# Two weight transfers issued earlier, a low-rank product in another PSUM bank, and one cast split over two engines

## The chip, the cores and the metric

The kernel runs on one core of one Trainium2 chip. The metric is the device time of one execution in microseconds (us), smaller is better. TensorE is called PE here (its weight loads PEld), VectorE DVE, ScalarE ACT, GpSimd POOL and SyncE SP. Each engine works through its own list of instructions in order; DMA transfers are issued from the lists of SP and POOL and run beside the engines.

## The reference

Two operators follow one another: a retention recurrence over 4 batches and 8 heads, and a mixer with a low-rank product over time and an MLP over channels.

```python
# q, k, v: (4, 8, 768, 64); gamma has one value for each head
for t in range(S):
    state = gamma[None, :, None, None] * state + einsum('bhd,bhe->bhde', k[:, :, t], v[:, :, t])
    y[:, :, t] = scale * einsum('bhd,bhde->bhe', q[:, :, t], state)
x = y.transpose(0, 2, 1, 3).reshape(B, S, H * D)          # (4, 768, 512)

xt = x.transpose(0, 2, 1)
h = xt @ U @ V                                            # U (768, 32), V (32, 768)
u = x + h.transpose(0, 2, 1)
out = u + relu(u @ w_ch1) @ w_ch2                         # w_ch1 (512, 2048), w_ch2 (2048, 512)
```

## The kernel before

The 768 steps of a batch are cut into six chunks of 128 (NCK is 6). Inside a chunk the recurrence is done as masked scores (k times q) multiplied with v, and across chunks as a running state multiplied with q. The powers of gamma are put on q and v when these are cast to bf16. Batch 0 has code of its own (the functions whose names end in `_early`) and works in three blocks of 256 steps, with q and k turned by PE. Batches 1 to 3 go by chunks, with q and k turned by DVE (`turn_chunk`, line 302). While PE does the MLP of batch b-1, the recurrence of batch b is put between the pieces of that MLP: `weave` takes a list of MLP pieces (`up`, line 452, and `down`, line 482) and a list of marks, each a share of the MLP at which a piece of other work is emitted.

The order on every engine is written out by hand: an engine executes its instructions in the order in which the Python code emits them. What the change and the steps of the prediction touch is this.

**Batch 0.** `cast_early` casts one block of q, k or v. Its last arguments say which engine takes which heads: ("P", 4, 4) gives heads 4 to 7 to POOL, ("D", 4, 4) gives them to DVE. `turn_early` then turns the block on PE (line 555) and copies it out of PSUM (`kt`, `qt`), `score_early` makes the scores (line 577) and masks them on DVE (`a`, line 582).

**The loads of batch 1.** All of them are issued by SP in this order: the first half of k (`kin`, eight transfers of 96 KB, line 107), the first half of q (`qin`), v of chunks 0 to 2 (256 KB each, line 116), the second half of k, and v of chunks 3 to 5. The second half of q has its eight transfers issued by POOL instead (line 107 too), in groups of 3, 3 and 2 between its casts. A half holds three chunks.

**The weights.** w_ch1 goes into the tile `w1b` in four transfers (`load_w1(0)` to `load_w1(3)`, line 280, 512 KB each as bf16), w_ch2 into `w2b` in four more (line 285). All eight are issued by POOL. `load_w1(0)` and `load_w1(1)` are issued during batch 0. The other two stand between the casts of batch 1's first chunk.

**The casts of batch 1.** POOL casts k (`ki`, line 83), q (`qi`, line 85) and v (`vd`, line 85) of each chunk, and each cast waits for the load of its data. In the order of before, POOL's list runs: the constants (lines 217 to 222), `ki` of chunk 0, `load_w1(2)`, `qi` of chunk 0, `load_w1(3)`, `vd` of chunk 0, `ki` and `qi` of chunk 1, three transfers of `qin`, `vd` of chunk 1, three more of `qin`, `ki`, `qi` and `vd` of chunk 2, two more of `qin`, two of `w2b`, `ki` of chunk 3, `qi` of chunk 3, and so on. `qi` of chunk 3 is the first that needs the second half of q.

**PSUM.** There are eight banks: `R[0]` and `R[1]` hold two each and carry scores, mixing and the low-rank product; three banks of the tag `mlp` are handed out in turn by `bank("mlp")`; one holds the state. `lr_proj(b)` multiplies x with U (24 matmuls, line 400) and copies the product `pc` out with DVE. Before the change it writes into the second bank of `R[1]`. In the first MLP, `lr_proj(1)` is emitted close behind `lr_expand(0, 0, 4)` (line 409), whose result in `R[0]` and `R[1]` is read by two additions on DVE (`u`, line 416).

Of the kernel before, what the change touches and what calls it, by code (L numbers as in the profile page):

```python
# [16 lines left out]
def kernel(  # L17
# [12 lines left out]
    P = 128  # L30
    B, H, S, D = q.shape
# [28 lines left out]
    R = [psum.tile([P, 2, 512], fp32, tag=f"r{g}", name=f"r{g}") for g in range(2)]  # L60

    def bank(tag, dtype=fp32):
        n_bank[0] += 1
        return psum.tile([P, 2048 // (4 if dtype == fp32 else 2)], dtype,
                         tag=tag, name=f"{tag}_{n_bank[0]}", bufs=BANKS[tag])
# [4 lines left out]
    def evac(eng, dst, src):  # L70
        if eng == "A":
            nc.scalar.activation(dst, src, AF.Copy)  # L72
        else:
            nc.vector.tensor_copy(out=dst, in_=src)

    def cast(eng, dst, src, scale=None):
        if eng == "A":
            assert scale is None
            nc.scalar.activation(dst, src, AF.Copy)
            return  # L80
        e = nc.vector if eng == "D" else nc.gpsimd
        if scale is None:
            e.tensor_copy(out=dst, in_=src)  # L83
        else:
            e.tensor_tensor(dst, src, scale, op=ALU.mult)  # L85
# [33 lines left out]
    def feed_more(n=0):  # L119
        allowed[0] += n  # L120
        while n_fed[0] < len(feed) and n_held[0] < RING and allowed[0] > 0:
            nm, b, i = feed[n_fed[0]]
            if nm == "T" and n_cast[b - 1] < NCK * (i + 1):
                return
            n_fed[0] += 1
            allowed[0] -= 1
            if nm == "T":
                load_turned("k", b, i)
                load_turned("q", b, i)
            else:  # L130
                load_natural(nm, b, i)
# [95 lines left out]
    def late_exps():  # L227
        nc.scalar.activation(gk, pos, AF.Exp, scale=-1.0)
        nc.scalar.activation(gqT, posT, AF.Exp)
# [3 lines left out]
    def prep_turned(nm, b, ci, eng="P"):  # L233
        src = turned_in[nm, b, ci // HC][:, :, ci % HC].rearrange("p h (a j d) -> p h a j d", a=2,
                                                   j=2)
        t = rpre.tile([P, 2, 2, D, 2], bf16, tag=nm + "i", name=f"{nm}i_{b}_{ci}")
        scale = None
        if nm == "q":
            scale = gqT[:, ci].rearrange("p h (a j) -> p h a j", a=2)
            scale = scale[:, :, :, :, None].to_broadcast([P, 2, 2, 2, D])  # L240
        cast(eng, t.rearrange("p h a d j -> p h a j d"), src, scale)
        pre[nm + "T", b, ci] = t
        n_cast[b] += 1
        feed_more()

    def prep_natural(nm, b, ci, eng="P"):
        t = rpre.tile([P, H, D], bf16, tag=nm + "d", name=f"{nm}d_{b}_{ci}")
        scale = None
        if nm == "v":
            scale = gk[:, ci, :, None].to_broadcast([P, H, D])  # L250
        cast(eng, t, take(nm, b, ci).rearrange("p (h d) -> p h d", h=H), scale)
        pre[nm, b, ci] = t
        feed_more()
# [25 lines left out]
    def load_w1(mb):  # L279
        nc.gpsimd.dma_start(  # L280
            out=w1b[:, :, ts(mb, 512)],
            in_=moe_w_ch1[:, ts(mb, 512)].rearrange("(c p) n -> p c n", p=P))
# [111 lines left out]
            pre.pop(("v", b, n))  # L394

    def lr_proj(b):
        p_p = R[1][:, 1]
        for j in range(NCK):
            for c in range(NCB):
                nc.tensor.matmul(p_p[ds(RK * c, RK), :P], Ub[:, j],  # L400
                                 xs[b][:, j, ts(c, P)], start=(j == 0),
                                 stop=(j == NCK - 1))
        pcs[b] = rmid.tile([P, P], bf16, tag="pc", name=f"pc_{b}")
        evac("D", pcs[b], p_p[:, :P])
# [128 lines left out]
    def home(shape, name):  # L533
        return rin.tile(shape, bf16, tag="in", name=name)
# [3 lines left out]
    def cast_early(nm, B0, *pieces):  # L538
        t = eb[nm, B0] = home([P, 2, H, D], f"{nm}b_{B0}")
        g = {"q": gq2, "k": None, "v": gk2}[nm]  # L540
        for eng, h0, nh in pieces:
            hs = ds(h0, nh)
            scale = None
            if g is not None:
                scale = g[:, B0, hs].rearrange("p h j -> p j h")
                scale = scale[:, :, :, None].to_broadcast([P, 2, nh, D])
            src = early[nm, B0][h0 // 4][:, ds(h0 % 4, nh)]
            cast(eng, t[:, :, hs], src.rearrange("p h (j d) -> p j h d", j=2), scale)

    def turn_early(nm, B0, engines="A"):  # L550
        src = eb[nm, B0]
        tp = bank("mlp", bf16)
        for hp in range(4):
            for j in range(2):
                nc.tensor.transpose(tp[:, ts(2 * hp + j, P)],  # L555
                                    src[:, j, ds(2 * hp, 2)], ident)
        t = eb[nm + "T", B0] = home([P, 4, 2 * P], f"{nm}t_{B0}")
        if nm == "k":
            evac(engines, t.rearrange("p n m -> p (n m)"), tp)
            return  # L560
        dst = t.rearrange("p n (t j) -> p n j t", j=2)
        src = tp.rearrange("p (n j t) -> p n j t", n=4, j=2)
        if len(engines) == 1:
            evac(engines, dst, src)
        else:
            for f in range(2):
                evac(engines[f], dst[:, ds(2 * f, 2)], src[:, ds(2 * f, 2)])
# [112 lines left out]
    state_early(3)  # L680
    load_w1(0)
    turn_early("q", 2)
    cast_early("k", 2, ("P", 0, 4), ("P", 4, 4))
    turn_early("k", 2, "D")
    cast_early("v", 2, ("P", 0, 4), ("D", 4, 4))
    load_uv()
# [14 lines left out]
    p_p = bank("mlp")  # L701
# [38 lines left out]
    for lo in range(2):  # L740
        for g in range(2):
            evac("AD"[g], uTs[0][:, ds(2 * g, 2), ts(lo, 256)], R[g][:, :, ts(lo, 256)])
    late_exps()
    prep_turned("k", 1, 0)
    load_w1(2)
    prep_turned("q", 1, 0)
    load_w1(3)
    prep_natural("v", 1, 0)
    prep_turned("k", 1, 1)
    prep_turned("q", 1, 1)  # L750
# [19 lines left out]
    for b in range(1, B):  # L770
# [22 lines left out]
        def mixed():  # L793
            if b > 1:
                lr_open(b)
            lr_proj(b)
# [41 lines left out]
```

## Time and profile before

| | us |
|---|---|
| median of 6 executions | 234.57 |
| lowest and highest of the 6 | 233.42 and 235.48 |
| the profiled execution, its own time | 234.04 |
| its span in the profile, first to last instruction | 232.3 |
| PE busy | 211.5 |
| DVE busy | 107.7 |
| POOL busy | 96.7 |
| ACT busy | 76.9 |
| mean granted TensorE clock | 0.993 of full |

The span is 1.7 us shorter than the time of the same execution; the rest lies outside the first and last instruction. All places in time below are counted from the start of the span. A line number such as L85 is a line of the kernel printed above, and `out<-in` after it names the tiles that an instruction writes and reads. A wait is written as "who waited <- who ended the wait". In a table of stretches (windows), the columns are the stretch, its length, the busy time of PE, PEld, DVE, ACT and POOL with the number of instructions in brackets, the granted TensorE clock as a share of full, the mean busy share of the 16 DMA engines (over 1 where packets overlap), and GB/s moved. A DMA's time "to landing" runs from its issue to the signal that its data is there.

### The profile page before, as it was taken

To read this page: it belongs to the slowest core of one execution; us is meant where nothing else is said; L and a number is where in the kernel's file an instruction comes from. 1 tells how busy PE (TensorE), PEld (TensorE's weight loads), DVE (VectorE), ACT (ScalarE), POOL (GpSimd) and SP (SyncE) were. 2 spreads that over 40 slices of the span, in tenths; PEclk is the share of its full clock that TensorE was granted. 3 is DMA by queue.
4 is the path that set the end of the run, shared out by engine and by line. 5 is a ranking of instruction groups with operands and counts; after the bars stand their busy time and mean duration, and the time that the engine had idled before them with its cause. 6 is when DMAs were issued, how large, how long until landed. Compare 5 with 4: busy or idle time off the path is not lost.

```text
span 232.3 us, 5794 instructions
## 1 busy us (share of the span) xinstructions
PE 211.5 (91%) x2411; PEld 123.0 (53%) x2437; DVE 107.7 (46%) x194; ACT 76.9 (33%) x174; POOL 96.7 (42%) x141
## 2 busy tenths in 40 slices
PE   0799799977979999999999999999999999999991
PEld 0577467635734444568644444577544444774451
DVE  5667546625566226765345255566416152222121
ACT  2355456653410005556320025566110044540000
POOL 4687559939502249199057401991011100001110
PEclk9999999997999999999999999999999999999999
DMA  6999979999942599997771768930023530001212
GB/s 175 290 291 235 262 178 223 273 207 233 228 133 93 130 222 254 217 250 193 180 148 45 181 180 211 259 86 0 3 93 81 144 90 0 3 0 45 93 61 74
DMA packets 65738, 35.21 MB, mean 152 GB/s; under 512 B 41920, under 2 KB 63808, under 8 KB 65712
## 3 DMA queue, kind: packets, MB, share of 16 engines
q1 hardware_dynamic: 59200, 23.64, 44.4%
q0 software_dynamic: 6512, 11.21, 19.4%
q8 instruction: 19, 0.31, 0.6%
q14 instruction: 7, 0.06, 0.1%
HBM read 30.90 MB, written 6.29 MB: 160 GB/s over the span
## 4 chain that ended last, share of the span: by engine, by line
PE 31%; issue 31%; DMA 13%; POOL 13%; SPq 9%; DVE 1%; POOLq 0%; DVEq 0%
PE mlp L482 15%; PE mlp L452 11%; DMA v<-in_v_dram 6%; DMA qin<-in_q_dram 4%; SPq L107 4%; POOL out_dram L441 3%; POOL qi L85 3%; SPq L163 3%; SPq L165 3%; DMA kin<-in_k_dram 3%; POOL vd L85 2%; POOL ki L83 2%; POOL qin L107 2%; PE r L369 1%; PE r L350 1%
## 5 line engine op out<-in xcount | busy, mean ns | idle before, releaser
L452 PE MATMUL mlp<-uT,w1b 128*128 128x256 bf16 (+1 forms) x517 | 89.0, 323 | 1.0 <-ACT uT L72 0.4
L482 PE MATMUL mlp<-w2b,gT 128*128 128x512 bf16 (+2 forms) x385 | 84.0, 370 | 1.5 <-issue 0.8
L459 ACT ACTIVATE gT<-mlp 128x256 bf16<-128x256 f32 (+1 forms) x90 | 42.8, 479 | 87.3 <-PE mlp L452 85.9
L452 PEld LDWEIGHTS <-w1b 128*128 128x128 bf16 x528 | 50.5, 99 | 31.7 <-issue 1.1
L482 PEld LDWEIGHTS <-gT 128*128 128x128 bf16 x400 | 37.4, 98 | 42.3 <-issue 0.4
L441 POOL DMA_DIRECT2D out_dram<-o x24 | 13.3, 556 | 93.1 <-DVE o L489 93.1
L489 DVE TENSOR_TENSOR o<-mlp,u 128x512 f32<-128x512 f32 (+2 forms) x25 | 16.7, 669 | 47.1 <-PE mlp L482 47.1
L384 DVE TENSOR_TENSOR a<-r,mask 128x512 bf16<-128x512 f32 x36 | 23.2, 686 | 25.3 <-ACT x L72 21.0
L457 DVE TENSOR_SCALAR gT<-mlp 128x256 bf16<-128x256 f32 (+1 forms) x42 | 22.8, 545 | 21.4 <-PE mlp L452 21.3
L85 POOL TENSOR_TENSOR qi<-qin,gqT 128x512 bf16<-128x512 f32 x18 | 18.9, 1048 | 3.6 <-DMA qin<-in_q_dram 3.6
L85 POOL TENSOR_TENSOR vd<-v,gk 128x512 bf16<-128x512 f32 x18 | 18.8, 1042 | 2.0 <-DMA v<-in_v_dram 0.7
L72 ACT ACTIVATE x<-r 128x256 bf16<-128x256 f32 x36 | 11.9, 381 | 23.3 <-PE r L369 14.8
L416 DVE TENSOR_TENSOR u<-r,x 128x512 bf16<-128x512 f32 (+1 forms) x16 | 14.6, 952 | 7.7 <-PE r L409 7.7
L83 POOL CAST kd<-k 128x512 bf16<-128x512 f32 x12 | 7.3, 609 | 19.6 <-DMA k<-in_k_dram 19.6
L83 POOL CAST ki<-kin 128x512 bf16<-128x512 f32 x18 | 13.8, 765 | 3.4 <-DMA qin<-in_q_dram 2.1
L369 PE MATMUL r<-qT,kT 32*128 32x128 bf16 x288 | 7.1, 215 | 2.9 <-DVE qT L302 2.9
L302 DVE STREAM_TRANSPOSE qT<-qi 128x256 f32<-128x256 f32 x18 | 7.3, 408 | 3.9 <-POOL qi L85 3.9
L302 DVE STREAM_TRANSPOSE kT<-ki 128x256 f32<-128x256 f32 x18 | 7.9, 437 | 2.3 <-POOL ki L83 2.3
L555 PE MATMUL mlp<-ident,qb 128*128 128x128 bf16 x24 | 3.5, 310 | 5.9 <-DVE qb L85 5.7
L350 PEld LDWEIGHTS <-a 128*128 128x128 bf16 x144 | 6.7, 100 | 2.4
L582 DVE TENSOR_TENSOR a<-r,mask 128x1024 bf16<-128x1024 f32 x6 | 7.1, 1219 | 1.2 <-PE r L577 1.2
L350 PE MATMUL r<-vd,a 128*128 128x64 bf16 x144 | 7.3, 196 | 0.0
(82 smaller groups left out, 131.3 us busy)
## 6 DMA issues: line engine op xcount, KB each, us to landing
v<-in_v_dram SPq DMA_DIRECT2D x24, 256.0 KB, 5.5
out_dram<-o POOLq DMA_DIRECT2D x23, 256.0 KB, 2.4
kin<-in_k_dram SPq DMA_DIRECT2D x48, 96.0 KB, 5.0
qin<-in_q_dram SPq DMA_DIRECT2D x40, 96.0 KB, 3.0
k<-in_k_dram SPq DMA_DIRECT2D x12, 256.0 KB, 4.8
w1b<-in_moe_w_ch_dram POOLq DMA_DIRECT2D x4, 512.0 KB, 8.7
w2b<-in_moe_w_ch_dram POOLq DMA_DIRECT2D x4, 512.0 KB, 10.4
qin<-in_q_dram SPq DMA_DIRECT2D x2, 512.0 KB, 5.8
```

What stands on the lines that cost most here:

```text
L83: e.tensor_copy(out=dst, in_=src)
L85: e.tensor_tensor(dst, src, scale, op=ALU.mult)
L302: nc.vector.transpose(out=dst, in_=src)
L350: nc.tensor.matmul(R[g][:, hp % 2, ds(256 + D * i, D)], a[:, 2 * hp + i], vb[:, 2 * hp + i], start=(i == 0), stop=True, skip_group_check=True)
L384: nc.vector.tensor_tensor(a[:, ds(4 * g, 4)].rearrange("p (n i) m -> p n i m", n=2), R[g][:, :, :256].rearrange("p n (i m) -> p n i m", i= ...
L416: nc.vector.tensor_tensor(v4(us[b][:, ds(j0, nj), e]), R[g][:, :, :nj * P].rearrange("p c (j e) -> p c j e", j=nj), v4(xs[b][:, ds(j0, nj) ...
L441: nc.gpsimd.dma_start(out=dst, in_=src)
L452: nc.tensor.matmul(g_p[:, :sz], w1b[:, c, ts(m, P)], uTs[b][:, c, ds(lo, sz)], start=(c == 0), stop=(c == NCB - 1))
L457: nc.vector.tensor_relu(gT[:, m, ds(lo, sz)], g_p[:, :sz])
L459: nc.scalar.activation(gT[:, m, ds(lo, sz)], g_p[:, :sz], AF.Relu)
L482: nc.tensor.matmul(ch[:, :nn], gT[:, m, ts(j, P)], w2b[:, m, ds(n0, nn)], start=(m == 0), stop=(m == NM - 1))
L489: nc.vector.tensor_tensor(o_sb, ch[:, :nn], us[b][:, j, n], op=ALU.add)
```

## The change

It has three parts, and none changes what is computed.

1. `load_w1(2)` is emitted ahead of `ki` of batch 1's chunk 0, and `load_w1(3)` ahead of `qi` of that chunk. Each moves forward past one cast on POOL's list.
2. `lr_proj` writes its product into a bank handed out by `bank("mlp")` in place of the second bank of `R[1]`. This holds for batches 1, 2 and 3.
3. The cast of k of batch 0's last block is split: heads 0 to 3 stay on POOL, heads 4 to 7 go to DVE.

```diff
     def lr_proj(b):
-        p_p = R[1][:, 1]
+        p_p = bank("mlp")
         for j in range(NCK):
             for c in range(NCB):
                 nc.tensor.matmul(p_p[ds(RK * c, RK), :P], Ub[:, j],
...
     turn_early("q", 2)
-    cast_early("k", 2, ("P", 0, 4), ("P", 4, 4))
+    cast_early("k", 2, ("P", 0, 4), ("D", 4, 4))
     turn_early("k", 2, "D")
...
     late_exps()
+    load_w1(2)
     prep_turned("k", 1, 0)
-    load_w1(2)
+    load_w1(3)
     prep_turned("q", 1, 0)
-    load_w1(3)
     prep_natural("v", 1, 0)
```

## The prediction

> **What bounds the kernel now.** I read the page first, then PE's waits, then the chain of waits from 24 to 60 us, then POOL in order of time, then the DMA load by stretches.
>
> ```profile
> span 232.3 us, 5794 instructions
> PE 211.5 (91%) x2411; PEld 123.0 (53%) x2437; DVE 107.7 (46%) x194; ACT 76.9 (33%) x174; POOL 96.7 (42%) x141
> ```
>
> PE is busy 91% of the span, so time is gained only where PE waits. Its waits between 20 and 75 us:
>
> ```profile
> PE r L369 <- DVE qT L302: 2.9, 1, 2.9
> PE r L400 <- DVE u L416: 1.5, 1, 1.5
> ```
>
> These are the two largest once the start is over, and after 75 us the waits of PE itself come to 0.6 us. So parts 1 and 3 matter only through what comes before the first MLP and through the 2.9, part 2 through the 1.5. Where the 2.9 comes from is told by the chain:
>
> ```profile
> 31.20 3.66 DMA v<-in_v_dram
> 34.86 0.08 issue
> 34.95 1.03 POOL vd L85
> ...
> 44.76 0.52 POOL qin L107
> 45.29 6.57 DMA qin<-in_q_dram
> ...
> 52.16 1.05 POOL qi L85
> 53.22 0.02 issue
> 53.24 0.46 DVE qT L302
> 53.70 0.04 issue
> 53.74 0.40 PE r L369 x16
> ```
>
> The load of v for chunk 0 lands, POOL then works without a hole from 34.95 until it has issued the last `qin` transfer at 45.29, that transfer takes 6.57, and `qi`, `qT` and PE follow. The lead of the chain is v of chunk 0. POOL around the moved transfers:
>
> ```profile
> 30.56 0.76 POOL L83 CAST ki<-kin 128x512 bf16<-128x512 f32 x1 [2.15 <-DMA qin<-in_q_dram]
> 31.24 0.82 POOL L280 DMA_DIRECT2D w1b<-in_moe_w_ch_dram  x1
> 32.90 1.04 POOL L85 TENSOR_TENSOR qi<-qin,gqT 128x512 bf16<-128x512 f32 x1 [0.85 <-DMA qin<-in_q_dram]
> 33.89 0.80 POOL L280 DMA_DIRECT2D w1b<-in_moe_w_ch_dram  x1
> 34.95 1.03 POOL L85 TENSOR_TENSOR vd<-v,gk 128x512 bf16<-128x512 f32 x1 [0.26 <-DMA v<-in_v_dram]
> ```
>
> It idles for 2.15, 0.85 and 0.26 us, each time for a load. The last columns of these stretches are DMA share and GB/s:
>
> ```profile
> 28.00:30.00 2.00, 1.63 (x16) 1.45 (x15) 1.17 (x3) 1.78 (x6) 0.35 (x2) 1.00 1.07 280
> 30.00:32.00 2.00, 2.00 (x23) 1.61 (x25) 0.74 (x2) 1.13 (x3) 1.44 (x2) 1.00 0.54 152
> 32.00:34.00 2.00, 1.95 (x18) 0.94 (x19) 1.65 (x3) 0.40 (x2) 1.15 (x3) 1.00 0.86 176
> 36.00:40.00 4.00, 4.00 (x52) 3.28 (x49) 3.05 (x7) 2.15 (x6) 3.98 (x6) 1.00 1.24 230
> ```
>
> The engines of the DMA have a lull at 30 to 34 us, and are full from 34 to 64 (1.1 to 1.3 in every stretch).
>
> **Part 2, the bank.** PE comes to L400 at 68.08 and starts it at 69.62, since the second addition `u`, which reads the bank, ends at 69.56. In an `mlp` bank the product need not wait: two of the three are held by the two open `down` products, the third was last read by a relu before 62 us, and x was copied out at 66.5. Gain 1.54. What is queued behind: the copy of `pc` (0.29) still stands behind `u` on DVE and ends near 69.9; `lr_expand`, the first to need it, would come at 70.4. The next `down` takes a free bank at 70.8; should it be given the first one, its sum `o` (0.69, after `pc`) is out at about 70.6. Next late is the last `w2b` transfer, landed at 66.63 and needed at 68.6, so 1.9 us of cover. Bounds: 0 if one of these takes over, -1.54 if none. I take -1.5, as each has a margin. For batches 2 and 3 nothing: PE has no wait at L400 there, and a free bank is used again no sooner than one whole `down` later (16 matmuls, over 3 us).
>
> **Part 3, the cast.** A half of k takes POOL about 0.59 (1.18 for two) and DVE 0.38 (0.76 for two in block 0). The second half ends at 19.48 on POOL now. On DVE it starts when the mask products end, 19.28, and is done at 19.66. PE's last four transposes come 0.2 later, as does `kt`: it would end at 21.05 and not 20.87. Behind it on DVE stands `vb`, which waits for its load until 21.18 (0.31 of idle), so the delay is covered. Without that cover it costs 0.2. POOL's 0.6 buys nothing, as its next cast, `vb` at 20.02, already waits 0.54 for a load. Bounds -0.1 to +0.2; I take 0.
>
> **Part 1, the transfers.** POOL is free at 28.41. `load_w1(2)` (0.82) moves from 31.24 to 28.41, into the hole of 2.15 ahead of `ki`; `load_w1(3)` (0.80) moves from 33.89 to 31.24, into the hole that is there ahead of `qi`. Neither delays a cast by its issue. `vd` is freed of 0.80 of issue ahead of it, but waits for v anyway, so POOL gains nothing. Nor does PE wait for `w1b` in the trace. What changes is the order of the data on the DMA engines:
>
> (a) A gain. The lull is filled: (1.2 - 0.54) x 2 + (1.2 - 0.86) x 2 = 2.0 us of share, over 1.2, or 1.7 us. All that is queued behind can land up to 1.7 earlier, the last `qin` included.
>
> (b) A loss. w1 would now move beside the end of q's first half and v of chunk 0, the head of the chain. The nearest rows are the v loads themselves, asked for one by one: v of chunk 0, issued at 31.20, lands in 3.7 us, before w1 gets going; v of chunk 1, issued at 31.70 and overlapped by `load_w1(2)`, takes 7.4; v of chunk 2, overlapped by both, 10.5. A v load is 262 KB, 1.0 us at the 250 GB/s of full stretches. So one w1 transfer delays a v load behind it by 7.4 - 3.7 - 1.0 = 2.7 us, two by about 10.5 - 3.7 - 2.0 = 4.8. In the new order v of chunk 0 would meet `load_w1(2)` after about a third of it has moved (issued 2.8 ahead of v), two thirds of 2.7 or about 2.0 us.
>
> Here a rule speaks against the change. The Trainium skill, "DMA: Bandwidth & Descriptors", Queues, rings and completion order, says that each DMA engine takes turns between the queues that have work, a packet at a time. Taking turns by descriptor, a v load has 1024 pieces of 256 B, w1 pieces of 1 KB; each piece of v would then wait for one of w1, all of both transfers, 1.05 MB or 4.2 us at 250 GB/s (an estimate from that page and the stretch rows), and the sum would be 2.2 higher than by the row. Taking turns by equal bytes, v waits for 262 KB, 1.0 us, and the sum is 1.0 lower. The row of v of chunk 1 lies between; I use it, and keep 0 and 4.8 as the ends.
>
> From v of chunk 0 on POOL has no hole, so 2.0 us late there is 2.0 late at the last `qin` issue. That transfer took 6.57 among full DMA engines (6.5 to 7.1 for all eight); with 1.7 us less queued it should take about 4.9. PE restarts 2.0 - 1.7 = 0.3 later. Bounds for the restart: -1.7 (no loss) to +4.8 (no gain); taken +0.3.
>
> **A second price on the same wait.** The stretch table by single microseconds gives a granted clock of 0.59, 0.50, 0.50 and 0.70 from 55 to 59 us, after the wait of 2.92: 1.7 us of full clock lost. The Trainium skill, "TensorE: Matmul & The Clock Gate", Part 1, lets the clock fall after an idle window of about 3.4 us; by that alone a wait of 2.9 costs no clock. The trace decides: it did, and the wait of 1.54 at 68 us did not. So with +0.3 the loss stays as it is and adds 0; were the wait cut to about 1.6, another 1.7 would come back (by the rule, nothing).
>
> **The sum.** -1.5 + 0 + 0.3 = -1.2. Against the profiled execution's 234.04 that is 232.8; it ran 0.5 under the median of 234.57, so on the median 233.4.
>
> **The rivals.** Half a percent, 1.17 us, is about what a measurement of this kernel can tell from no change: faster means under 233.4, slower over 235.7.
>
> A, likeliest, 0.45: as summed, 233.4, its own range 232.3 to 234.6; 0.20 faster, 0.23 same, 0.02 slower.
>
> B, 0.22, faster: v of chunk 0 is hardly touched, because its transfers are on their way before w1's are prepared. PE restarts 1.3 earlier: 231.8, and 230.1 if the clock no longer falls. For: `load_w1(2)` took 7.1 us to land, so it starts slowly. Against: it will be issued 2.8 us ahead of v.
>
> C, 0.25, slower: `load_w1(3)` follows `load_w1(2)` without a break, and v of chunk 0 gets through only behind both. It lands 4.8 late, near 39.7; POOL, and the `qin` issues on it, are late by that; less the 1.7, PE restarts 3.1 later: 234.57 - 1.5 + 3.1 = 236.2, and 237.9 with a second fall of the clock. It turns slower than the bound once the restart is over 2.7 late, that is, when v of chunk 0 lands after 39.3. For: the 10.5 of v of chunk 2. Against: the DMA can turn to v between the two. Chances 0.04 same, 0.21 slower.
>
> D, 0.08: part 2 gives nothing because the last `w2b` or a bank is late: 234.9; 0.06 same, 0.02 slower.
>
> Together 0.42 faster, 0.33 same, 0.25 slower. The range of 230.5 to 236.8 leaves out the best end of B and the worst of C.
>
> **What would show it.** Right: no wait at L400 near 68; `w1b` issues at 28.4 and 31.2; v of chunk 0 landing at 36 to 38 and `vd` following it; the last `qin` in about 5 us; PE's wait for `qT` near 3 us and the fall of the clock after it; `kt` 0.2 later with no trace on PE. Wrong: `vd` still at 35 (B), or after 39 (C), or a wait for a bank or `w2b` at 68 to 71 (D), or a PE wait after 75 us that is not there now.

## The result and the profile after

By its ratio to the kernel before, 1.0002 with a 95% interval of 0.998 to 1.0024, the change makes no difference that the measurement can tell. The median of all 35 executions is 236.17 us, against 234.45 of 72 of the kernel before. The ratio is formed from the executions within 1.5% of the fastest of their own kernel (14 of the 35, 63 of the 72), so it leaves out most of the long ones, of which the changed kernel has more: 21 of its 35 took over 236 us, against 4 of the 72.

The profiled execution took 232.52 us, the shortest of the 35. It shows what the change can do at its best. The page and PE's waits between 20 and 75 us:

```profile
span 230.7 us, 5794 instructions
PE 213.0 (92%) x2411; PEld 123.7 (54%) x2437; DVE 108.0 (47%) x195; ACT 77.1 (33%) x174; POOL 96.1 (42%) x140
```

```profile
PE r L369 <- DVE qT L302: 2.3, 1, 2.3
PE mlp L452 <- ACT uT L72: 0.4, 1, 0.4
PE mlp L314 <- DVE kT L302: 0.2, 1, 0.2
...
```

The wait of 1.5 us at L400 is gone, the wait for `qT` is still there. POOL in order of time, around the moved transfers:

```profile
28.50 0.81 POOL L280 DMA_DIRECT2D w1b<-in_moe_w_ch_dram  x1
30.94 0.76 POOL L83 CAST ki<-kin 128x512 bf16<-128x512 f32 x1 [1.62 <-DMA kin<-in_k_dram]
31.62 0.77 POOL L280 DMA_DIRECT2D w1b<-in_moe_w_ch_dram  x1
35.89 1.05 POOL L85 TENSOR_TENSOR qi<-qin,gqT 128x512 bf16<-128x512 f32 x1 [3.50 <-ACT uT L72]
36.90 1.04 POOL L85 TENSOR_TENSOR vd<-v,gk 128x512 bf16<-128x512 f32 x1
```

Both issues sit in holes, as intended. But `qi` of chunk 0 starts at 35.89 and not at 32.90, and `vd` at 36.90 and not at 34.95. The name behind the 3.50 (ACT `uT`, done long before) is not what ended that wait: the last transfers of q's first half landed only at 35.8, by their issue and landing times in the trace, where they had landed at 32.8. The load of v of chunk 0 took 5.4 us (3.7 before) and was in at 36.7, while POOL was still at `qi`: here it is q, not v, that holds `vd` back.

The load of the DMA engines, with share and GB/s in the last two columns, shows the lull filled:

```profile
30.00:32.00 2.00, 2.00 (x20) 1.67 (x18) 0.85 (x2) 1.02 (x3) 1.06 (x2) 1.00 1.04 189
32.00:34.00 2.00, 1.95 (x17) 0.92 (x17) 1.54 (x3) 0.52 (x2) 0.39 (x1) 1.00 1.17 219
```

The end of the chain to PE's restart, and then the place of the product, from the chain of waits:

```profile
47.22 4.72 DMA qin<-in_q_dram
...
52.25 1.05 POOL qi L85
53.30 0.02 issue
53.32 0.46 DVE qT L302
53.78 0.04 issue
53.82 0.40 PE r L369 x16
```

```profile
67.36 0.81 PE mlp L482 x3
68.17 0.45 PE mlp L400 x24
68.62 1.83 PE mlp L482 x8
```

The last `qin` transfer is issued 1.9 us later than before and takes 4.72 in place of 6.57, so PE restarts at 53.82 against 53.74: 0.1 later. The product follows the matmuls before it without a hole. In this execution 0.1 is lost and 1.5 gained, and the span is 1.6 shorter. The question is why most executions do not keep that.

### The profile page after: what moved, and what is told of

Same layout as the page of the kernel before. It is cut to its first block, busy times and chain, and to the rows that moved or that the text cites. A ratio compares the mean times of both kernels' runs of the same rounds, so it can differ in the third digit from the quotient of the medians.

```text
span 230.7 us, 5794 instructions
## 1 busy us (share of the span) xinstructions
PE 213.0 (92%) x2411; PEld 123.7 (54%) x2437; DVE 108.0 (47%) x195; ACT 77.1 (33%) x174; POOL 96.1 (42%) x140
## 4 chain that ended last, share of the span: by engine, by line
PE 35%; issue 30%; SPq 15%; DMA 9%; POOL 7%; DVE 2%; POOLq 0%; ACT 0%; DVEq 0%
PE mlp L452 13%; PE mlp L482 13%; SPq L107 7%; DMA u<-in_k_dram 3%; POOL out_dram L441 3%; SPq L116 2%; DMA qin<-in_q_dram 2%; SPq L163 2%; SPq L424 2%; DMA kin<-in_k_dram 2%; SPq L165 2%; POOL qi L85 2%; DMA v<-in_v_dram 2%; POOL vd L85 1%; PE r L369 1%
## 5 line engine op out<-in xcount | busy, mean ns | idle before, releaser
L459 ACT ACTIVATE gT<-mlp 128x256 bf16<-128x256 f32 (+1 forms) x90 | 42.8, 479 | 86.0 <-PE mlp L452 84.7
```

The source lines that it names most:

```text
L459: nc.scalar.activation(gT[:, m, ds(lo, sz)], g_p[:, :sz], AF.Relu)
```

## The experiments

### Each part alone

Part 2 alone (`e1_bank`), part 1 alone (`e2_w1`), parts 2 and 3 (`e3_bank_cast`), and part 3 alone (`e9_cast`), each against the kernel before. The diffs are the pieces of the change shown above.

Part 2 alone:

> Part 2 alone (the product in a bank of its own). Theory G (given back: the bank saves its 1.5 us, and the earlier weight transfers cost about as much in the timed executions, though they cost 0.1 in the profiled one): ratio 0.992 to 0.996, and no wait at L400. Rival N (the bank saves nothing at the end, because a later wait takes its place, and the transfers are neutral): 0.998 to 1.002, with a new PE wait after 70 us. Rival K (bank and transfers as predicted, but the split cast costs over 1 us): 0.992 to 0.996 here too.

Measured: ratio 0.9952 (0.9924 to 0.9979), median 233.19 of 22 executions against 234.16. There is no wait at L400 in its list of PE's waits, and none takes its place after 70 us. The first line of that list from 20 to 75 us:

```profile
PE r L369 <- DVE qT L302: 1.8, 1, 1.8
```

So the bank is worth about 1.1 us (0.48% of 234.16), inside what theory G gave and somewhat under the 1.5 that one trace shows; that 1.5 is inside the interval. Rival N is out.

Part 1 alone:

> Part 1 alone (load_w1(2) ahead of the k cast, load_w1(3) ahead of the q cast). Theory G: slower, ratio 1.004 to 1.012, the wait of 1.5 us at L400 back, and in the profile v of chunk 0 landing at 36 us or later. Rival N: 0.998 to 1.002. Rival K: 0.999 to 1.003.

Measured: ratio 1.0072 (1.0037 to 1.0107), median 237.14. POOL in order of time:

```profile
28.85 0.81 POOL L280 DMA_DIRECT2D w1b<-in_moe_w_ch_dram  x1
31.04 0.76 POOL L83 CAST ki<-kin 128x512 bf16<-128x512 f32 x1 [1.38 <-DMA kin<-in_k_dram]
31.72 0.77 POOL L280 DMA_DIRECT2D w1b<-in_moe_w_ch_dram  x1
35.93 1.04 POOL L85 TENSOR_TENSOR qi<-qin,gqT 128x512 bf16<-128x512 f32 x1 [3.44 <-DMA qin<-in_q_dram]
37.33 1.04 POOL L85 TENSOR_TENSOR vd<-v,gk 128x512 bf16<-128x512 f32 x1 [0.35 <-DMA v<-in_v_dram]
```

Here the profile names the loads: `qi` waits 3.44 us for q, then `vd` 0.35 more for v, which lands at 37.2. The wait at L400 is back at 1.5 us. Part 1 costs 1.7 us by the ratio (0.72% of 234.16; 0.9 to 2.5 by the interval) and 3.0 by the medians of all executions (237.14 against 234.16). By the ratios the two parts nearly cancel. By the medians they do not: -1.0 and +3.0 us, and the whole change +1.7. Either way part 1 gives back at least about what part 2 gains, and theory G stands.

Parts 2 and 3:

> Parts 2 and 3 without part 1. Theory G: as part 2 alone within 0.2%, ratio 0.992 to 0.996. Rival N: 0.998 to 1.002. Rival K: about 1.000, that is 0.4% or more over part 2 alone, with the masks of the last block later on DVE by over 1 us.

Measured: 0.9972 (0.9947 to 0.9998), median 232.89. The ratio is 0.2% over that of part 2 alone, the median 0.3 us under it, and the intervals overlap over more than half of their width. No difference from part 2 alone is shown.

Part 3 alone:

> Part 3 alone. Theory: nothing, ratio 0.998 to 1.002, since DVE's cast ends 0.2 us later than POOL's did and vb on DVE waits for its load anyway. Rival K (the split cast costs): 1.002 to 1.005, the masks of the last block on DVE starting over 0.3 us later than the load of v explains.

Measured: 0.9999 (0.9972 to 1.0026). No effect of the cast shows, and of rival K's range (1.002 to 1.005) all but the lowest end lies outside the interval.

### Which of the two transfers

`e4_one_w1` puts `load_w1(3)` back behind the q cast, `e10_w1_3_early` puts `load_w1(2)` back behind the k cast. Both keep parts 2 and 3.

```diff
     load_w1(2)
     prep_turned("k", 1, 0)
-    load_w1(3)
     prep_turned("q", 1, 0)
+    load_w1(3)
```

> The changed kernel with load_w1(3) put back behind the q cast: only load_w1(2) is early. Theory G with its cause in the second transfer (v of chunk 0 gets through only behind both): faster, ratio 0.992 to 0.996, v of chunk 0 landing at 35 to 37 us. Theory G with its cause in load_w1(2) alone: 0.998 to 1.003, as the whole change. Rival N: 0.998 to 1.002.

Measured: 1.0116 (1.0072 to 1.016), median 236.58 of 6. None of the expectations held: with one early transfer fewer, it is no faster than the whole change. By the ratio it is slower; the medians of all executions (236.58 of these 6, 236.17 of the 35) are too near to show that. Its POOL and PE:

```profile
36.16 1.04 POOL L85 TENSOR_TENSOR qi<-qin,gqT 128x512 bf16<-128x512 f32 x1 [4.22 <-ACT uT L72]
37.15 0.81 POOL L280 DMA_DIRECT2D w1b<-in_moe_w_ch_dram  x1
37.98 1.05 POOL L85 TENSOR_TENSOR vd<-v,gk 128x512 bf16<-128x512 f32 x1
```

```profile
PE r L369 <- DVE qT L302: 4.8, 1, 4.8
```

`load_w1(2)` alone makes q's first half late (`qi` at 36.16). `load_w1(3)` now stands behind that late `qi` and is issued at 37.15, where it was at 33.89. It is under way until about 45, beside the first six transfers of q's second half, which take 7.0 to 8.5 us (5.3 to 6.0 in the profile of the whole change). The last `qin`, issued at 48.29 when `load_w1(3)` had landed, still took 7.5 us; what slowed that one is not shown. Nothing of the lateness is won back.

```diff
-    load_w1(2)
     prep_turned("k", 1, 0)
+    load_w1(2)
     load_w1(3)
     prep_turned("q", 1, 0)
```

> The changed kernel with load_w1(2) put back behind the k cast, so that only load_w1(3) is early (directly behind load_w1(2), ahead of the q cast). Theory V2 (load_w1(2), which starts before v of chunk 0 is on its way, does the harm): v of chunk 0 lands at about 35 us as before, ratio 0.992 to 0.998. Rival V3 (the two in one row do it, wherever the first stands): v of chunk 0 lands after 37, ratio 0.999 to 1.008.

Measured: 1.0012 (0.9979 to 1.0045). POOL:

```profile
33.47 1.05 POOL L85 TENSOR_TENSOR qi<-qin,gqT 128x512 bf16<-128x512 f32 x1 [0.34 <-DMA qin<-in_q_dram]
39.01 1.04 POOL L85 TENSOR_TENSOR vd<-v,gk 128x512 bf16<-128x512 f32 x1 [4.49 <-DMA v<-in_v_dram]
```

Now q is in time and v of chunk 0 is late, by 4 us: it takes 7.2 us and lands at 38.9. That is rival V3. So each of the two moves makes a load late: the first q's first half, the second, by putting both transfers in one row, v of chunk 0. In time the second is a borderline case: its ratio is 0.4% over that of parts 2 and 3 without part 1 (0.9972), and the two intervals overlap.

### Two more profiles of the changed kernel

The profile at hand came from the shortest execution, so the same kernel was profiled twice more.

> The changed kernel, unaltered, for one more profile. Theory G (part 1 makes q's first half and v of chunk 0 late by 2 to 3 us in every execution, and how much of it the second half of q gains back varies): vd of chunk 0 starts between 36 and 40 us; PE's wait for qT between 2 and 6 us, longer than in the profile at hand (2.3) if this execution takes longer. Rival F (vd of chunk 0 itself is late by a varying amount, because the second w1 transfer follows the first without a break in some executions): vd of chunk 0 over 39 us where the time is over 235.

> As the look before, a second one. Theory G: vd of chunk 0 between 36 and 38 us whatever the time, and the time from the last qin issue to its landing between 4.7 and 8 us, longer where the execution takes longer. Rival F: vd of chunk 0 later by as much as the execution is longer.

They took 237.67 and 236.15 us. POOL and PE's waits of the first:

```profile
36.49 1.05 POOL L85 TENSOR_TENSOR qi<-qin,gqT 128x512 bf16<-128x512 f32 x1 [4.30 <-DMA qin<-in_q_dram]
39.71 1.04 POOL L85 TENSOR_TENSOR vd<-v,gk 128x512 bf16<-128x512 f32 x1 [2.17 <-DMA v<-in_v_dram]
```

```profile
PE r L369 <- DVE qT L302: 3.7, 2, 3.4
PE mlp L314 <- DVE kT L302: 2.3, 2, 1.8
```

`vd` starts at 39.71 and, in the second profile, at 38.80; the last `qin` takes 7.07 and 6.45. Both are later or longer than in the shortest execution (36.90 and 4.72), so theory G, which held the start of `vd` to be 36 to 38 whatever the time, is wrong there. Rival F is right that v itself is late by a varying amount, but only in part: `vd` is 2.8 and 1.9 later where the executions are 5.2 and 3.6 longer, and the end of the chain varies too. These are single executions and say nothing of how often each comes. They do account for their own times. The stretches of the first show the granted clock in the third column from the end:

```profile
48.00:52.00 4.00, 3.73 (x66) 2.08 (x68) 2.32 (x5) 2.13 (x5) 4.00 (x6) 0.75 1.21 213
52.00:56.00 4.00, 3.60 (x39) 1.73 (x37) 0.45 (x1) 1.64 (x3) 0.89 (x2) 0.82 1.17 228
60.00:64.00 4.00, 4.00 (x38) 3.05 (x39) 2.67 (x6) 1.51 (x6) 4.00 (x5) 0.57 1.19 253
```

PE's waits for `kT` and `qT` are 6.0 us in this profile, against 2.9 before. The clock falls to half twice, each time for about 3.4 us, at 50 to 53.5 and at 60 to 64, where it fell once before; one fall costs about 1.7 us of full clock. The sum is 234.04 + 3.1 + 1.7 - 1.5 = 237.3. In the second, 4.7 us of such waits and again two falls give 234.04 + 1.8 + 1.7 - 1.5 = 236.0.

### v ahead of q

If the price were v stuck behind w1, SP could load v of chunk 0 first.

```diff
+    load_natural("v", 1, 0)
     load_turned("q", 1, 0)
-    for ci in range(HC):
+    for ci in range(1, HC):
         load_natural("v", 1, ci)
```

> The whole change, with v of chunk 0 loaded by SP ahead of q's first half and not behind it. Theory V (part 1's price is v of chunk 0 getting through only behind both w1 transfers, landing at 38.7 to 39.7 us in the two looks): v of chunk 0 lands before 36, vd follows qi without a wait, PE restarts 2 to 4 us earlier than in the looks, ratio 0.992 to 1.000. Rival Q (the lateness of q's first half, 35 to 36 us, already costs as much): as the whole change or worse, 1.000 to 1.012.

Measured: 1.0141 (1.0105 to 1.0178), the highest ratio of all and over what rival Q gave; the median is 237.26 of 6. POOL:

```profile
38.94 1.05 POOL L85 TENSOR_TENSOR qi<-qin,gqT 128x512 bf16<-128x512 f32 x1 [6.12 <-DMA v<-in_v_dram]
39.95 1.04 POOL L85 TENSOR_TENSOR vd<-v,gk 128x512 bf16<-128x512 f32 x1
```

The name behind the 6.12 (v, in at 32.9) is not what ended that wait: q's first half, now behind v, lands at 38.7. Its last transfer is issued at 32.9 (30.8 in the order of the whole change) and takes 5.8 us. So theory V falls in its narrow form. It is not v that is at fault: whatever stands last among the loads of chunk 0 is late, with both w1 transfers under way beside it, and all of them have to be in before POOL can go on.

### The issues of q's second half moved forward

`e5_qin_early` is part 2 alone with POOL's eight `qin` issues moved forward past casts; `e6_w1_qin_early` has the same and the whole change.

```diff
     prep_natural("v", 1, 0)
+    load_turned("q", 1, 1, nc.gpsimd, range(3))
     prep_turned("k", 1, 1)
     prep_turned("q", 1, 1)
-    load_turned("q", 1, 1, nc.gpsimd, range(3))
-    prep_natural("v", 1, 1)
     load_turned("q", 1, 1, nc.gpsimd, range(3, 6))
-    prep_chunk(1, 2)
-    load_turned("q", 1, 1, nc.gpsimd, range(6, 8))
+    prep_natural("v", 1, 1)
+    load_turned("q", 1, 1, nc.gpsimd, range(6, 7))
+    prep_turned("k", 1, 2)
+    prep_turned("q", 1, 2)
+    load_turned("q", 1, 1, nc.gpsimd, range(7, 8))
+    prep_natural("v", 1, 2)
```

> Part 2 alone, and the eight POOL issues of q's second half moved forward past casts (three ahead of ki of chunk 1, three ahead of vd of chunk 1, one ahead of ki of chunk 2, the last ahead of vd of chunk 2; w1 where it was before). Theory P (the last qin issue, and POOL's chain in front of it, sets PE's restart): last qin issue near 44 us and not 45.3 to 46, PE's wait for qT 0.5 to 1.7 us in place of 1.8 to 2.9, ratio 0.985 to 0.993. Rival L (the load of the DMA engines sets it, whenever the issue comes): the transfers only take longer, wait within 0.4 us of part 2 alone, ratio 0.993 to 0.998.

Measured: 0.9896 (0.9866 to 0.9926), median 231.13. The ratio is as theory P has it, the profile only in part. The last issue is at 45.02, held up by another thing:

```profile
45.02 0.60 POOL L107 DMA_DIRECT2D qin<-in_q_dram  x1 [0.44 <-DMA w1b<-in_moe_w_ch_dram]
```

It waits for a w1 transfer, `load_w1(3)`, the eighth before it on POOL, which was issued at 34.37 and took 10.4 us. PE's wait for `qT` is still 2.3 us, and 0.8 is waited for a `w2b` transfer, but the clock does not fall in this stretch in this profile, which is worth 1.7 us against part 2 alone. So the gain in the timed executions is shown, and the way to it that theory P gives, a shorter wait for `qT`, is not.

> The whole change, and the POOL issues of q's second half moved forward as in the run before. Theory P: part 1's price comes through POOL's chain, so much of it goes when the issues no longer stand at the end of that chain: 0.3 to 0.8% over the run without part 1, ratio 0.988 to 0.998. Rival L: the price is unchanged, 0.7 to 1.2% over the run without part 1. Rival U (with the lull filled and the issue early, part 1 is a gain): under the run without part 1 by 0.2% or more.

Measured: 0.9957 (0.9929 to 0.9985). This run has part 3 too, for which no effect was seen. Part 1 costs about 0.6% here (0.9957 against 0.9896), near the 0.7% without the move. That is inside what theory P expected, but it can't be told from rival L. Rival U is out: part 1 is no gain in this setting either.

### The contrary of part 1

`e8_w1_late` is part 2 alone, with `load_w1(3)` moved back, behind `vd` of chunk 0 and the first three `qin` transfers. It moves POOL's `qin` issues forward as well, so it is not a test of the w1 transfer alone.

```diff
     prep_turned("q", 1, 0)
-    load_w1(3)
     prep_natural("v", 1, 0)
+    load_turned("q", 1, 1, nc.gpsimd, range(3))
+    load_w1(3)
     prep_turned("k", 1, 1)
     prep_turned("q", 1, 1)
-    load_turned("q", 1, 1, nc.gpsimd, range(3))
-    prep_natural("v", 1, 1)
     load_turned("q", 1, 1, nc.gpsimd, range(3, 6))
+    prep_natural("v", 1, 1)
+    load_turned("q", 1, 1, nc.gpsimd, range(6, 8))
     prep_chunk(1, 2)
-    load_turned("q", 1, 1, nc.gpsimd, range(6, 8))
```

> Part 2 alone, and the contrary of part 1: load_w1(3) moved back behind vd of chunk 0 and the first three transfers of q's second half, the other five of these in a group of three ahead of vd of chunk 1 and a group of two ahead of ki of chunk 2. Theory P (what is needed first should be issued first, and the last qin issue sets the restart): last qin issue at 42 to 44 us, landing before 50, PE's wait for qT under 1.5 us, ratio 0.980 to 0.990. Rival W (w1 then comes too late for PE, or its issue collides with q's second half): a new PE wait of over 1 us for w1b at 46 to 50, or qin landing as before, ratio 0.990 to 1.000.

Measured: 0.9866 (0.9814 to 0.9919), median 231.14 of 6 executions. POOL:

```profile
34.37 1.04 POOL L85 TENSOR_TENSOR vd<-v,gk 128x512 bf16<-128x512 f32 x1
35.36 1.73 POOL L107 DMA_DIRECT2D qin<-in_q_dram  x3
37.06 0.79 POOL L280 DMA_DIRECT2D w1b<-in_moe_w_ch_dram  x1
...
42.21 1.16 POOL L107 DMA_DIRECT2D qin<-in_q_dram  x2
...
50.03 1.04 POOL L85 TENSOR_TENSOR qi<-qin,gqT 128x512 bf16<-128x512 f32 x1
```

`vd` of chunk 0 runs at 34.37, the last `qin` issue begins at 42.8, and `qi` of chunk 3 at 50.03, two us ahead of before. PE's list of waits from 20 to 75 us no longer has a line for `qT`, and none for `w1b`: in this profile issuing the weights later costs PE nothing. That is theory P's case, and rival W is out. Against the profile before, the span is 4.6 shorter (227.7 to 232.3), and the two waits of 2.9 and 1.5 are nearly all of it; the clock falls once in both. This and `e5_qin_early` beat both the kernel before and the changed one; their intervals overlap, so which of them is the better is open, and with it whether the later w1 adds anything to the earlier `qin` issues.

## Why the prediction was wrong

**Part 2, the bank.** Right in mechanism: the wait at L400 is gone, no bank and no `w2b` is late, and no new wait follows. The size taken was -1.5; part 2 alone measured -1.1 (0.5 to 1.8 by its interval).

**Part 3, the cast.** Right: taken as 0, measured 0.9999, and in the changed kernel's profile `kt` ends at 21.07, 0.2 later than before, as expected.

**Part 1, the transfers.** This is the step that failed, and in it the term "PE restarts 2.0 - 1.7 = 0.3 later". Part 1 alone measured +1.7. Both of its terms come out at their size in the shortest execution, the 2.0 by luck, and not in the two further profiles, where PE restarts at 58.97 and 57.44, 5.2 and 3.7 later than before.

The 2.0 was read from v of chunk 1, on the argument that v of chunk 0 would meet only two thirds of one w1 transfer (two thirds of 2.7 are 1.8). The argument put `load_w1(3)` at nothing, though by the prediction's own times it would be issued at 31.24, beside v at 31.20. The row itself was a fair price for one transfer: with only `load_w1(2)` early (`e4_one_w1`), v of chunk 0 took 5.4 us, 1.7 more than before. With both early it took 5.4 in the shortest execution, 5.7 in part 1 alone, and 8.0 and 7.9 in the two further profiles. The start of `vd` on POOL moved by +1.95 in the shortest execution and +2.4 in part 1 alone, but by +4.1 with only the second transfer early and by +3.9 and +4.8 in the two further profiles. In these two, v landed only 0.4 us ahead of `load_w1(3)` (39.7 and 40.1, 38.8 and 39.2), so it got through about when both had, as rival C had it; in the shortest execution it landed 2.8 ahead (36.7 and 39.5). What decides between the two is open.

The estimate that the prediction drew, by descriptor, from the rule of turns (the Trainium skill, "DMA: Bandwidth & Descriptors", Queues, rings and completion order) was 4.2, and it was set aside for the row; the last three of these shifts fall around it, the first two around the row. The page has turns by packet; that a packet of either stream holds as many pieces is the estimate's own assumption, and no run here shows it. A row for one transfer was not enough to set an estimate for both aside.

The statement that neither issue delays a cast was true of the issues and missed the data: `qi` of chunk 0 starts 2.5 to 3.6 later in every profile with `load_w1(2)` early and the loads in their old order (35.4 to 36.5 us), for q's first half was still on its way when w1 began. The prediction named "the end of q's first half" and then priced v alone. In the shortest execution q was all that mattered: `vd` started directly behind the late `qi`, so that its 1.95 agrees with the predicted 2.0 of v by luck.

The 1.7 to be won back was found in the shortest execution (the last `qin` took 4.72 and not 6.57) but not in the further profiles (7.07 and 6.45). A filled lull moves the same bytes earlier; it does not say whose. Those that came earlier were w1's, and PE waits for no `w1b` in any of these profiles. And PE waits in a second place that the prediction's path lacks: 2.3 and 1.8 us for `kT` in the further profiles, where the profile before has no such wait.

**The clock.** The prediction expected the fall of the clock to go once the wait was about 1.6. After the wait of 1.8 in part 2 alone (with 0.5 for `kT` before it) the granted clock was 0.67 in the stretch from 52 to 56 us; after the 2.3 of `e5_qin_early` it stayed full. So the length of the wait alone did not decide it here. Nor does the rule of an idle window of about 3.4 us (the Trainium skill, "TensorE: Matmul & The Clock Gate", Part 1) describe these profiles, since falls came with waits of 1.8 to 2.9 us. What else decides was not tried.

**The outcome.** -1.1 and +1.7 with their intervals give a sum around zero, and the whole change measured 1.0002. The forecast of 233.4 was case A, which the one profiled execution met closely (232.52, with 232.8 forecast for it); the two further ones (236.15 and 237.67, both with a second fall of the clock) were near case C, which had 236.2, and 237.9 with such a fall. The likeliest case was drawn too near to the good end of a term whose ends lay 6.5 us apart. How often each meeting of the transfers comes was not counted.

## What to carry to other kernels

A lull of the DMA engines just ahead of a critical load is no free room: a transfer put there can still be under way when that load is issued, and make it late. Price such a move by what lands next on the critical engine's list, all of it and not only the last item, and weigh whether anything waits for what was moved. Here nothing did, and the two kernels that issued the critical loads earlier instead, and no w1 transfer earlier (one of them a w1 transfer later), were the fastest. And when one execution is profiled, ask which one it was: here a term that depends on how two streams of transfers meet varied between executions, and the shortest showed its good end.

## What the runs showed of the hardware

A transfer of 512 KB issued by POOL made the loads beside it late by more than its own bytes need. With only `load_w1(2)` early, the last transfer of q's first half took 4.8 us to land where it had taken 2.1, so 2.7 more, though 512 KB are 2.1 us at the 250 GB/s of full stretches (an estimate). In `e7_v_first`, with both early and v ahead of q, that transfer of 96 KB took 5.8 us.

A POOL issue can wait for an earlier POOL transfer to land (the eighth before it on POOL: 0.44 us for a `w1b` transfer in `e5_qin_early`, 0.34 for a `qin` in `e4_one_w1`), so in these kernels a slow transfer can hold up issues that don't need its data. Whether the program or the chip asks for this wait is not shown.

In the profile of `e8_w1_late` the granted clock was 0.60 and 0.55 in the stretches from 28 to 32 us, where the kernel before, with much the same holes in PE's work ahead of it (3.0 us busy of the four from 24 to 28 in both), kept full clock: much the same load did not get the same clock.
